# One float32 product per score tile, and one softmax and transpose group per pair, in the attention of a fused attention and two-layer expert kernel

## The chip, the cores and the metric

The kernel runs on one core of a Trainium2 chip. The core has a matrix engine (TensorE, in the rows PE, with its weight loads as PEld), a vector engine (DVE), an activation engine (ACT), GpSimd (POOL) and a queue engine (SP) that issues most transfers. The metric is device time in microseconds (us) for one launch; lower is better.

## The reference

The inputs are q, k and v of 8 batches, 8 heads, 576 positions and 64 channels in float32, and five weight matrices.

```
k_p = mean of k over groups of 8 positions      # 576 -> 72 keys
v_p = mean of v over groups of 8 positions
scores = q @ k_p.T / 8                          # per batch and head: 576 x 72
attn = softmax(scores)                          # over the 72 pooled keys
x = (attn @ v_p), heads side by side            # 4608 tokens x 512
h = max(x @ w1, x @ w2, x @ w3)                 # 4608 x 768
y = h @ w_out                                   # 4608 x 512
out = (max(y @ w_in, 0) ** 2) @ w_out2          # 2048 hidden units
```

## The kernel before

The work has two stages. The first holds the attention and the three-expert layer (`moe1`), for 12 blocks of 384 tokens (`T1`). The second, from about 776 us on, is the squared layer and is not touched by the change.

All large products are made from float32 numbers split into a high and a low part of a shorter type, float32r (`F32R`); a product of two split operands is three products of parts (`PARTS`). A `split` is a copy to float32r on ACT and a subtraction on DVE or POOL. `moe1(j)` issues 22 steps for block j (`STEPS`): 18 steps of 12 products of 384 columns (L487), then 4 steps of 18 products (L506). Three PSUM banks (`mm_ps`) take turns as their targets.

The attention of block j+1 is laid between the steps of block j. A block has pieces: the part of one batch in it, of 384 or 192 tokens (`n`). For each piece and each of the 4 pairs of heads, `attend` gives five functions, and `attention` puts each at a time in `todo`, counted in steps: `load` 10 steps ahead, `prepare` 4 steps ahead, `softmax`, then `transpose` 3 steps later (`LAG_T`), then `values` 3 steps after the last transpose (`LAG_V`). The list is sorted and recorded in that order, and a scheduler then sets each engine's own order. A piece of 384 tokens has 3 score tiles of 128 tokens, one of 192 has 2 tiles of 96 (`score_tiles`). Over the kernel there are 96 tiles of 128 and 64 tiles of 96.

- Batch 0 (`whole`, `b < NATURAL`): the scores are one float32 product a tile with `kbd_f` (L356).
- Batches 1 to 7: `prepare` splits q into `qs` and the pooled keys into `kbd` (L203), and a tile's scores are three float32r products of 144 columns (L360).
- In blocks 0 and 1 (`LIGHT`) all tiles of a piece go through one `softmax` group; in blocks 2 to 11 each tile is a group of its own.
- `softmax`: the maximum (DVE, L362), an exponential with its sum for each tile and head (ACT, L365), a sum guard and a reciprocal (DVE), and the scaling (POOL, L371).
- `transpose`: both heads of one tile are transposed on TensorE into one tile `tr` of its own PSUM bank, and written to `pt` by ACT (L396, high part) and DVE (L397, low part).
- `values`: each head's products with the pooled values go to the banks `av0` and `av1` (L417, L418), and x is formed and split.

Before the first steps can run at full rate, 18 tiles of `w1` and 6 of `wo1` are loaded and turned from 64-bit to float32 by two ACT and two DVE operations each (`wbits`, L149 to L154), and then split. Later blocks do the same for the second stage's weights.

Of the kernel before, what the change touches and what calls it, by code (L numbers as in the profile page):

```python
# [20 lines left out]
P = 128  # L21
# [47 lines left out]
LIGHT = 2  # L69
# [16 lines left out]
def attention_moe_kernel(ctx: ExitStack, tc: tile.TileContext, q, k, v, vn, w1, w2, w3, wo1, wi2, wo2, out):  # L86
# [90 lines left out]
    qs_p = s_at.enter_context(tc.tile_pool(name="qs_p", bufs=2, side="right"))  # L177
# [8 lines left out]
    kbd = kv_p.tile([P, NPAIR, 2, 2, SP], F32R, name="kbd")  # L186

    vst = kv_p.tile([SP, NPAIR, 4, D], F32R, name="vst")

    kbd_f = kv_p.tile([P, NPAIR, 2, SP], F32, name="kbd_f")  # L190
    nc.gpsimd.memset(kbd_f, 0.0)
# [5 lines left out]
    nc.gpsimd.memset(as_f32(kbd), 0.0)  # L197
# [28 lines left out]
    def prepare_k(b, p, kr):  # L226
        ks = sm_p.tile([P, SP], F32, tag="ks", name="ks", bufs=2)
        nc.vector.tensor_reduce(out=ks, in_=kr.rearrange("p (a b) -> p a b", b=POOL), axis=AX.X, op=ALU.add)
        for h in range(2):
            r = slice(h * D, (h + 1) * D)  # L230
            if b < NATURAL:
                nc.scalar.activation(kbd_f[r, p, h], ks[r], AF.Copy, scale=K_SCALE)
            else:
                split_scaled(kbd[r, p, 0, h], kbd[r, p, 1, h], ks[r], K_SCALE)
# [48 lines left out]
    def attention(j):  # L283

        x_t[j] = [None] * NPAIR
        n_tiles = sum(NPAIR * len(score_tiles(n)) for _, _, n, _ in pieces(j))
        pace = (STEPS - 1) / n_tiles
        at = (j - 1) * STEPS + pace / 2 - (LAG_T + LAG_V + LEAD_X)
        for b, s0, n, t in pieces(j):
            if s0 == 0 and b < NATURAL:  # L290
                tiles = []
                when = at - pace / 2 + LAG_T + LAG_V if t else at + pace / 2
                todo.append((when - LEAD_LOAD, lambda b=b, tiles=tiles: tiles.extend(load_natural(b))))
                todo.append((when, lambda tiles=tiles: pool_v(tiles)))
            for p in range(NPAIR):
                load, prepare, softmax, transpose, values = attend(j, b, s0, n, p, t)
                todo.append((at - LEAD_LOAD, load))
                todo.append((at - LEAD_PREP, prepare))
                tiles = score_tiles(n)
                if j < LIGHT:  # L300
                    todo.append((at, functools.partial(softmax, tiles)))
                for c, m in tiles:
                    if j >= LIGHT:
                        todo.append((at, functools.partial(softmax, [(c, m)])))
                    todo.append((at + LAG_T, functools.partial(transpose, c, m)))
                    at += pace
                todo.append((at - pace + LAG_T + LAG_V, values))
# [10 lines left out]
    def attend(j, b, s0, n, p, t):  # L318

        kr, vr, qr, qs, pt, sms = [], [], [], [], [], {}  # L320
        first, light, whole = s0 == 0, j < LIGHT, b < NATURAL

        def load():
# [7 lines left out]
            if j:  # L331
                qr.append(raw_p.tile([P, T1], F32, tag="qr", name="qr", bufs=2)[:, :n])
# [4 lines left out]
        def prepare():  # L337
            if first:
                prepare_k(b, p, kr[0])
            if whole:  # L340
                return
            qs.append(qs_p.tile([P, 2, T1], F32R, tag="qs", name="qs")[:, :, :n])
            split(qs[0], qr[0], nc.gpsimd if light else nc.vector)

        def softmax(tiles):

            c, m = tiles[0]
            if vr and (light or c == m):
# [5 lines left out]
            for i, (c, _) in enumerate(tiles):  # L354
                if whole:
                    nc.tensor.matmul(src[:, i], lhsT=qr[0][:, c : c + m], rhs=kbd_f[:, p], start=True, stop=True)  # L356
                    continue
                hi, lo = qs[0][:, 0, c : c + m], qs[0][:, 1, c : c + m]
                for n, (lhsT, l) in enumerate(((hi, 0), (hi, 1), (lo, 0))):
                    nc.tensor.matmul(src[:, i], lhsT=lhsT, rhs=kbd[:, p, l], start=(n == 0), stop=(n == 2))  # L360
# [14 lines left out]
            for i, (c, _) in enumerate(tiles):  # L375
                sms[c] = ss[:, i]

        def transpose(c, m):
            if c == 0 and whole:
                pt.append(pt_p.tile([SP, 2, T1], F32, tag="pt", name="pt"))  # L380
            elif c == 0:
                pt.append(pt_p.tile([SP, 2, 2, T1], F32R, tag="pt", name="pt"))
            if light and c == m:
                tr = av_ps.tile([P, T1], F32, tag="av1", name="tr")[:SP, : 2 * P].rearrange("s (h q) -> s h q", h=2)
            else:
                tr = tr_ps.tile([SP, 2, P], F32, tag="tr", name="tr")
            for h in range(2):
                nc.tensor.transpose(tr[:, h, :m], sms[c][:, h], ident[:m, :m])  # L388
            if whole:
                if p % 2:  # L390
                    nc.vector.tensor_copy(pt[0][:, :, c : c + m], tr[:, :, :m])
                else:
                    nc.scalar.activation(pt[0][:, :, c : c + m], tr[:, :, :m], AF.Copy)
                return
            hi, lo = pt[0][:, 0, :, c : c + m], pt[0][:, 1, :, c : c + m]
            nc.scalar.activation(hi, tr[:, :, :m], AF.Copy)  # L396
            nc.vector.tensor_tensor(out=lo, in0=tr[:, :, :m], in1=as_f32(hi), op=ALU.subtract)  # L397
# [355 lines left out]
```

## Time and profile before

| what | value |
|---|---|
| time, median of 3 runs | 1535.58 us (1532.88 to 1535.72) |
| profiled execution, first to last instruction (its span) | 1532.5 us |
| median beside that span | 3.1 us more |
| TensorE matmuls busy | 1502.5 us (98%) |
| DVE busy | 943.6 us (62%) |
| ACT busy | 618.6 us (40%) |
| POOL busy | 192.8 us (13%) |
| mean granted TensorE clock | 0.991 of full speed |

No time of the profiled execution is listed apart from its span; what the chip needs around it is read as the 3.1 us between the span and the median. "Busy" is a mean over the whole span; matmuls overlap in the pipeline, so a matmul's own duration is longer than the distance to the next one, and the distance is what counts for the rate.

### The profile page before, as it was taken

How to read it: one execution, taken by the hardware profiler on the slowest of the kernel's cores; microseconds unless marked ns; L12 is line 12 of the kernel's file. 1: busy time of each engine (PE TensorE's matmuls, PEld its weight loads, DVE VectorE, ACT ScalarE, POOL GpSimd, SP SyncE). 2: the span in 40 equal slices, each digit the busy share in tenths (PEclk: the TensorE clock that was granted, in tenths of full speed). 3: DMA queues.
4: the chain of work that ended last, by engine and by line, in shares of the span. 5: the costliest groups of instructions: out<-in, count | busy, mean ns of one | idle time of the engine just before them, and what ended most of it. 6: DMA issues, size and time to landing. Idle time of an engine off the chain costs nothing.

```text
span 1532.5 us, 25029 instructions
## 1 busy us (share of the span) xinstructions
PE 1502.5 (98%) x9254; PEld 1407.0 (92%) x9254; DVE 943.6 (62%) x1971; ACT 618.6 (40%) x1756; POOL 192.8 (13%) x329
## 2 busy tenths in 40 slices
PE   6889999999999999999999999999999999999998
PEld 4779999999999999999999899988999988999987
DVE  5897577776777766854427456464656555564644
ACT  6785466665666556654212112121212112121211
POOL 3551022222222221212000000000000000000000
PEclk8899999999999999999999999999999999999999
DMA  6553134333344333323485434333333433243321
GB/s 208 182 162 92 62 105 154 133 105 136 127 132 137 110 120 98 118 76 113 136 307 195 152 111 165 110 128 126 105 138 130 145 124 135 84 154 110 137 111 69
DMA packets 80858, 200.86 MB, mean 131 GB/s; under 512 B 9024, under 2 KB 32576, under 8 KB 80736
## 3 DMA queue, kind: packets, MB, share of 16 engines
q1 hardware_dynamic: 73824, 189.83, 36.3%
q10 hardware_dynamic: 6912, 9.44, 1.8%
q8 instruction: 73, 1.20, 0.3%
q14 instruction: 49, 0.40, 0.1%
HBM read 157.29 MB, written 41.94 MB: 130 GB/s over the span
## 4 chain that ended last, share of the span: by engine, by line
PE 88%; DVE 5%; DMA 3%; ACT 2%; issue 1%; SPq 0%; POOL 0%; ACTq 0%; DVEq 0%; POOLq 0%
PE acc L669 26%; PE ps L487 25%; PE ps L624 23%; PE ps L506 9%; PE sc L360 2%; PE tr L388 2%; DMA wraw<-in_wo_dram 1%; PE av L418 1%; PE av L417 1%; DVE wbits L151 1%; DVE wbits L154 1%; DMA wraw<-in_w_dram 1%; ACT ss L365 1%; DMA kq<-in_k_dram 1%; DMA vr<-in_v_dram 0%
## 5 line engine op out<-in xcount | busy, mean ns | idle before, releaser
L487 PE MATMUL ps<-x,w 128*128 128x384 f32 x2592 | 504.6, 342 | 2.1 <-DVE hm L495 1.7
L487 PEld LDWEIGHTS ps<-x,w 128*128 128x128 f32 x2592 | 448.7, 190 | 4.7 <-ACT wbits L149 2.0
L669 PE MATMUL acc<-wo2s,g 128*128 128x512 f32 x1728 | 411.0, 391 | 0.0
L624 PEld LDWEIGHTS ps<-y,wi2s 128*128 128x128 f32 x3024 | 368.9, 188 | 8.4 <-DVE c L641 0.5
L624 PE MATMUL ps<-y,wi2s 128*128 128x256 f32 x3024 | 374.1, 280 | 0.5 <-DVE c L641 0.3
L669 PEld LDWEIGHTS acc<-wo2s,g 128*128 128x128 f32 x1728 | 316.7, 188 | 62.9
L122 ACT ACTIVATE g<-c 128x512 fp32r<-128x512 f32 x144 | 90.7, 630 | 409.0 <-DVE c L635 399.7
L641 DVE TENSOR_TENSOR s<-ps,s 128x512 f32<-128x512 f32 x72 | 49.8, 691 | 253.7 <-PE ps L624 253.5
L506 PE MATMUL ps<-h,wo 128*128 128x384 f32 x864 | 168.1, 342 | 3.0 <-DVE st L369 0.9
L506 PEld LDWEIGHTS ps<-h,wo 128*128 128x128 f32 x864 | 149.9, 190 | 4.4 <-POOL wo L123 2.0
L371 POOL TENSOR_TENSOR ss<-ss,st 128x144 f32<-128x144 f32 (+3 forms) x144 | 71.4, 497 | 383.9 <-DVE st L370 297.7
L495 DVE TENSOR_TENSOR hm<-ps,hm 128x384 f32<-128x384 f32 x144 | 79.6, 553 | 60.6 <-PE ps L487 58.0
L641 DVE TENSOR_TENSOR c<-ps,s 128x512 f32<-128x512 f32 x144 | 99.0, 688 | 27.7 <-PE ps L624 24.4
L123 DVE TENSOR_TENSOR g<-c,g 128x512 fp32r<-128x512 f32 x144 | 98.7, 686 | 23.6 <-ACT g L122 22.9
L365 ACT ACTIVATE ss<-sc,st 128x72 f32<-128x72 f32 (+1 forms) x320 | 98.4, 314 | 35.2 <-DVE st L362 33.5
L635 DVE SCALAR_TENSOR_TENSOR c<-c 128x512 f32<-128x512 f32 x144 | 98.9, 688 | 2.2
L592 POOL COPY t<-g 1x1 f32<-1x1 f32 x32 | 8.4, 304 | 692.8 <-DVE g L123 692.8
L397 DVE TENSOR_TENSOR pt<-tr,pt 72x256 fp32r<-72x256 f32 (+1 forms) x140 | 54.0, 386 | 41.1 <-ACT pt L396 40.4
L396 ACT ACTIVATE pt<-tr 72x256 fp32r<-72x256 f32 (+1 forms) x140 | 49.3, 353 | 61.4 <-PE tr L388 59.6
L360 PE MATMUL sc<-kbd,qs 128*128 128x144 f32 (+1 forms) x420 | 65.1, 261 | 0.6 <-ACT ss L365 0.6
L362 DVE TENSOR_REDUCE st<-sc 128x2 f32<-128x144 f32 (+3 forms) x144 | 45.4, 316 | 32.9 <-PE sc L360 25.1
L122 ACT ACTIVATE h<-hm 128x384 fp32r<-128x384 f32 x72 | 37.7, 523 | 68.8 <-DVE hm L495 68.1
(84 smaller groups left out, 1349.5 us busy)
## 6 DMA issues: line engine op xcount, KB each, us to landing
wo2s<-wo_dram SPq DMA_DIRECT2D x144, 512.0 KB
wi2s<-wi_dram SPq DMA_DIRECT2D x24, 512.0 KB
wraw<-in_wo_dram SPq DMA_DIRECT2D x22, 512.0 KB
wraw<-in_w_dram SPq DMA_DIRECT2D x18, 512.0 KB
y_dram<-ys ACTq DMA_DIRECT2D x48, 192.0 KB
out_dram<-o SPq DMA_DIRECT2D x36, 256.0 KB
wraw<-in_wi_dram SPq DMA_DIRECT2D x16, 512.0 KB
wi_dram<-wraw SPq DMA_DIRECT2D x16, 512.0 KB
```

The lines of the kernel that those rows point to most:

```text
L122: nc.scalar.activation(hi, src, AF.Copy)
L123: engine.tensor_tensor(out=lo, in0=src, in1=as_f32(hi), op=ALU.subtract)
L360: nc.tensor.matmul(src[:, i], lhsT=lhsT, rhs=kbd[:, p, l], start=(n == 0), stop=(n == 2))
L365: nc.scalar.activation(ss[:, i, h], src[:, i, h], AF.Exp, bias=st[:, 0, i, h : h + 1], accum_out=st[:, 1, i, h : h + 1],)
L371: nc.gpsimd.tensor_tensor(out=ss, in0=ss, in1=st[:, 2].rearrange("p g (h o) -> p g h o", o=1).to_broadcast([m, g, 2, SP]), op=ALU.mult,)
L487: nc.tensor.matmul(ps, lhsT=w1_t[f, e][:, a, kk * P : (kk + 1) * P], rhs=x[kk][:, c], start=(n == 0), stop=(n == 3 * KD - 1),)
L495: nc.vector.tensor_tensor(out=hm, in0=ps, in1=hm, op=ALU.max)
L506: nc.tensor.matmul(ps, lhsT=wo1_t[kk][:, a, d * P : (d + 1) * P], rhs=hs[kk][:, c], start=(n == 0), stop=(n == 3 * KF1 - 1),)
L624: nc.tensor.matmul(bank[:, u * HT : (u + 1) * HT], lhsT=wi2_t[2 * gr + u][i][:, a, o + kk * P : o + (kk + 1) * P], rhs=y_t[j][m][:, c, kk] ...
L635: nc.vector.scalar_tensor_tensor(out=c, in0=c, scalar=0.0, in1=c, op0=ALU.max, op1=ALU.mult)
L641: nc.vector.tensor_tensor(out=c, in0=bank, in1=other, op=ALU.add)
L669: nc.tensor.matmul(acc_t[j][2 * half + i], lhsT=g[:, a, u * HT + i * P : u * HT + (i + 1) * P], rhs=wo2_t[j, 4 * gr + 2 * u + h][:, c], st ...
```

## The change

Every score tile, of every batch, is now one float32 product of q and the pooled keys as they stand; the splits of q (`qs`) and of the keys (the low part of `kbd`) are gone, and with them the pool `qs_p` and one of the two key tiles. q tiles (`qr`) are held until the scores are made and have four buffers in place of two. In all blocks the 3 or 2 tiles of a piece are one softmax group. The transposes of a piece are made together, head by head: head 0 of all tiles into the bank of `tr`, head 1 of all tiles into the bank that the value products of head 1 (`av1`) also use. Each head is then evicted to `pt` by one ACT and one DVE operation over the whole piece.

```diff
-    kbd = kv_p.tile([P, NPAIR, 2, 2, SP], F32R, name="kbd")
-    kbd_f = kv_p.tile([P, NPAIR, 2, SP], F32, name="kbd_f")
-    nc.gpsimd.memset(kbd_f, 0.0)
+    kbd = kv_p.tile([P, NPAIR, 2, SP], F32, name="kbd")
+    nc.gpsimd.memset(kbd, 0.0)
...
-            if b < NATURAL:
-                nc.scalar.activation(kbd_f[r, p, h], ks[r], AF.Copy, scale=K_SCALE)
-            else:
-                split_scaled(kbd[r, p, 0, h], kbd[r, p, 1, h], ks[r], K_SCALE)
+            nc.scalar.activation(kbd[r, p, h], ks[r], AF.Copy, scale=K_SCALE)
...
-                tiles = score_tiles(n)
-                if j < LIGHT:
-                    todo.append((at, functools.partial(softmax, tiles)))
-                for c, m in tiles:
-                    if j >= LIGHT:
-                        todo.append((at, functools.partial(softmax, [(c, m)])))
-                    todo.append((at + LAG_T, functools.partial(transpose, c, m)))
-                    at += pace
+                todo.append((at, softmax))
+                todo.append((at + LAG_T, transpose))
+                at += pace * len(score_tiles(n))
                 todo.append((at - pace + LAG_T + LAG_V, values))
...
-                qr.append(raw_p.tile([P, T1], F32, tag="qr", name="qr", bufs=2)[:, :n])
+                qr.append(raw_p.tile([P, T1], F32, tag="qr", name="qr", bufs=4)[:, :n])
...
-            if whole:
-                return
-            qs.append(qs_p.tile([P, 2, T1], F32R, tag="qs", name="qs")[:, :, :n])
-            split(qs[0], qr[0], nc.gpsimd if light else nc.vector)
...
-                if whole:
-                    nc.tensor.matmul(src[:, i], lhsT=qr[0][:, c : c + m], rhs=kbd_f[:, p], start=True, stop=True)
-                    continue
-                hi, lo = qs[0][:, 0, c : c + m], qs[0][:, 1, c : c + m]
-                for n, (lhsT, l) in enumerate(((hi, 0), (hi, 1), (lo, 0))):
-                    nc.tensor.matmul(src[:, i], lhsT=lhsT, rhs=kbd[:, p, l], start=(n == 0), stop=(n == 2))
+                nc.tensor.matmul(src[:, i], lhsT=qr[0][:, c : c + m], rhs=kbd[:, p], start=True, stop=True)
...
-        def transpose(c, m):
+        def transpose():
...
             for h in range(2):
-                nc.tensor.transpose(tr[:, h, :m], sms[c][:, h], ident[:m, :m])
...
+                if h:
+                    tr = av_ps.tile([P, T1], F32, tag="av1", name="tr")[:SP, :n]
+                else:
+                    tr = tr_ps.tile([SP, T1], F32, tag="tr", name="tr")[:, :n]
+                for i, (c, _) in enumerate(tiles):
+                    nc.tensor.transpose(tr[:, c : c + m], sms[0][:, i, h], ident[:m, :m])
+                if not whole:
+                    hi, lo = pt[0][:, 0, h, :n], pt[0][:, 1, h, :n]
+                    nc.scalar.activation(hi, tr, AF.Copy)
+                    nc.vector.tensor_tensor(out=lo, in0=tr, in1=as_f32(hi), op=ALU.subtract)
+                elif h:
+                    nc.vector.tensor_copy(pt[0][:, h, :n], tr)
+                else:
+                    nc.scalar.activation(pt[0][:, h, :n], tr, AF.Copy)
```

On TensorE, in the middle of the first stage (`sc` are scores, `tr` transposes, `ps` the products of `moe1`), before stands this:

```order
L487 MATMUL ps<-x,w_3_0_522 128x384 x4
L487 MATMUL ps<-x,w_3_1_543 128x384 x12
L360 MATMUL sc<-kbd,qs 128x144 x3
L487 MATMUL ps<-x,w_3_2_566 128x384 x4
L388 MATMUL tr<-ident,ss 72x128 x2
L487 MATMUL ps<-x,w_3_2_566 128x384 x8
L487 MATMUL ps<-x,w_4_0_595 128x384 x12
L360 MATMUL sc<-kbd,qs 96x144 x3
```

And with the change, in such a stretch of a like block:

```order
L465 MATMUL ps<-x,w_1_1_412 128x384 x12
L367 MATMUL tr<-ident,ss 72x128 x3
L465 MATMUL ps<-x,w_1_2_422 128x384 x12
L339 MATMUL sc<-kbd,qr 128x144 x3
L465 MATMUL ps<-x,w_2_0_445 128x384 x4
L367 MATMUL tr<-ident,ss 72x128 x3
L465 MATMUL ps<-x,w_2_0_445 128x384 x8
```

The three scores in a row were the parts of one tile and are now the three tiles of a piece; two transposes (the heads of a tile) are now three (one head of the three tiles).

On DVE, at the end of the conversion of the first layer's weights (`wbits`; the last row of either fence is the last of these 48 operations; `kbd` and `qs` are the splits of keys and q, `st` the softmax statistics), before stands this:

```order
L228 TENSOR_REDUCE ks<-kr 128x72
L151 SCALAR_TENSOR_TENSOR wbits<-wbits,wraw 128x512
L362 TENSOR_REDUCE st<-sc 128x2
L369 TENSOR_SCALAR st<-st 128x2
L123 TENSOR_TENSOR qs<-qr,qs 128x384
L238 TENSOR_REDUCE vs<-vr 72x128
L421 TENSOR_TENSOR xf<-av_1178,xf 64x192
L362 TENSOR_REDUCE st<-sc 128x2
L397 TENSOR_TENSOR pt<-tr,pt 72x2x128
L203 SCALAR_TENSOR_TENSOR kbd<-ks,kbd 64x72 x2
L154 SCALAR_TENSOR_TENSOR wbits<-wraw,wbits 128x512
```

And with the change:

```order
L230 TENSOR_REDUCE vs<-vr 72x128
L348 TENSOR_SCALAR st<-st 128x6
L153 SCALAR_TENSOR_TENSOR wbits<-wraw,wbits 128x512
L223 TENSOR_REDUCE ks<-kr 128x72
L399 TENSOR_TENSOR xf<-av_1203,xf 64x192
L349 RECIPROCAL st<-st 128x6
L371 TENSOR_TENSOR pt<-tr,pt 72x384
L150 SCALAR_TENSOR_TENSOR wbits<-wbits,wraw 128x512
L230 TENSOR_REDUCE vs<-vr 72x128
L122 TENSOR_TENSOR x<-xf,x 128x192
L153 SCALAR_TENSOR_TENSOR wbits<-wraw,wbits 128x512
```

The splits of keys and q are gone from between the conversions, the statistics come for six columns at a time, and more of the later attention (the x of a piece, the transposes' eviction) has moved ahead of the last conversion. Ahead of the last weight split on ACT stand 70 exponentials before and 80 with the change, and 8 copies of q to float32r before and none with the change.

On TensorE with the change, in a block of 192-token pieces, this is a stretch between two uses of the `av1` bank (`av1_2734` is a value product of head 1, `tr_2778` the transposes of head 1 of a later pair; both lie in that bank):

```order
L396 MATMUL av1_2734<-pt_2562,vst_168 128x192
L465 MATMUL ps_2828<-x_2238,w1_2_0_445 128x384 x3
L465 MATMUL ps_2828<-x_2402,w1_2_0_445 128x384 x3
L339 MATMUL sc_2846<-kbd_169,qr_2483 96x144 x2
L465 MATMUL ps_2870<-x_1944,w1_2_1_476 128x384 x3
L465 MATMUL ps_2870<-x_2087,w1_2_1_476 128x384 x3
L465 MATMUL ps_2870<-x_2238,w1_2_1_476 128x384 x3
L465 MATMUL ps_2870<-x_2402,w1_2_1_476 128x384 x3
L465 MATMUL ps_2887<-x_1944,w1_2_2_486 128x384 x2
L367 MATMUL tr_2778<-ident_63,ss_2666 72x96 x2
```

Between the last value product and the first transpose stand 20 products of 384 columns and two score products. Before, from block 2 on, `av1` held value products alone and the transposes took turns in the bank of `tr`.

## Rows read from the trace of the kernel before

**Rows 1.** Busy time, share of the span, instructions, by engine.

```profile
PE 1502.5 (98%) x9254; PEld 1407.0 (92%) x9254; DVE 943.6 (62%) x1971; ACT 618.6 (40%) x1756; POOL 192.8 (13%) x329
```

**Rows 2.** Three stretches: busy PE, PEld, DVE, ACT, POOL; clock, DMA share, GB/s.

```profile
0.00:140.00 140.00, 115.46 (x585) 99.01 (x586) 108.47 (x230) 100.92 (x335) 59.05 (x64) 0.90 0.56 172
140.00:754.00 614.00, 613.21 (x3789) 605.48 (x3788) 416.78 (x1089) 360.49 (x1160) 125.34 (x233) 1.00 0.35 117
754.00:1532.00 778.00, 773.84 (x4884) 702.55 (x4882) 418.31 (x652) 157.22 (x262) 8.45 (x32) 1.00 0.38 135
```

**Rows 3.** All that TensorE waited for, 140 to 725 us (total, times, longest).

```profile
PE tr L388 <- DVE pt L397: 0.7, 2, 0.4
```

**Rows 4.** Stretches of 10 us, 90 to 120 us, columns as in group 2.

```profile
90.00:100.00 10.00, 7.97 (x47) 7.33 (x46) 9.97 (x20) 7.42 (x21) 4.89 (x5) 1.00 0.49 156
100.00:110.00 10.00, 8.37 (x46) 6.84 (x44) 9.34 (x21) 8.53 (x26) 6.78 (x5) 1.00 0.49 137
110.00:120.00 10.00, 7.11 (x35) 5.80 (x35) 9.84 (x23) 6.96 (x29) 4.03 (x4) 0.85 0.42 114
```

**Rows 5.** Of what TensorE waited for, 0 to 140 us, one row.

```profile
PE ps L487 <- DVE hm L495: 1.7, 1, 1.7
```

**Rows 6.** TensorE groups by shape: busy, mean ns of one, idle before.

```profile
L360 PE MATMUL sc<-kbd,qs 128*128 128x144 f32 x252 | 41.6, 268 | 0.6 <-ACT ss L365 0.6
L360 PE MATMUL sc<-kbd,qs 128*96 128x144 f32 x168 | 23.5, 250 | 0.0
```

**Rows 7.** TensorE in order of time, three stretches: start, length, instructions.

```profile
195.10 2.32 PE L487 MATMUL ps<-x,w 128*128 128x384 f32 x12
197.26 0.45 PE L360 MATMUL sc<-kbd,qs 128*128 128x144 f32 x3
197.54 2.31 PE L487 MATMUL ps<-x,w 128*128 128x384 f32 x12
...
248.12 2.29 PE L487 MATMUL ps<-x,w 128*128 128x384 f32 x12
250.25 0.40 PE L360 MATMUL sc<-kbd,qs 128*96 128x144 f32 x3
250.48 1.26 PE L487 MATMUL ps<-x,w 128*128 128x384 f32 x6
...
734.85 29.39 PE L487 MATMUL ps<-x,w 128*128 128x384 f32 x168
```

**Rows 8.** TensorE in order of time, two groups of float32 scores.

```profile
15.73 0.90 PE L356 MATMUL sc<-kbd_f,kq 128*128 128x144 f32 x6
...
40.33 0.65 PE L356 MATMUL sc<-kbd_f,qr 128*96 128x144 f32 x4
```

**Rows 9.** The float32 scores' durations, min, median, max in ns.

```profile
L356 PE MATMUL sc<-kbd_f,kq x24: 286/286/580, 6.3 to 20.6; 128*128 128x144 f32 x24
```

**Rows 10.** DVE groups by shape, 0 to 125 us.

```profile
L203 DVE SCALAR_TENSOR_TENSOR kbd<-ks,kbd 64x72 fp32r<-64x72 f32 x12 | 5.8, 485 | 0.2
L123 DVE TENSOR_TENSOR qs<-qr,qs 128x384 fp32r<-128x384 f32 x5 | 3.4, 686 | 0.0
```

**Rows 11.** ACT in order of time: the exponentials of one tile.

```profile
307.04 0.32 ACT L365 ACTIVATE ss<-sc,st 128x72 f32<-128x72 f32 x1
...
307.35 0.31 ACT L365 ACTIVATE ss<-sc,st 128x72 f32<-128x72 f32 x1
```

**Rows 12.** DVE groups by shape, whole span.

```profile
L362 DVE TENSOR_REDUCE st<-sc 128x6 f32<-128x432 f32 x4 | 2.4, 608 | 5.7 <-PE sc L356 5.7
...
L238 DVE TENSOR_REDUCE vs<-vr 72x128 f32<-72x1024 f32 x28 | 33.9, 1211 | 3.4 <-DMA vr<-in_v_dram 3.0
...
L421 DVE TENSOR_TENSOR xf<-av,xf 64x384 f32<-64x384 f32 x56 | 31.0, 554 | 9.5 <-ACT xf L420 7.6
```

**Rows 13.** POOL's scaling of a group of three tiles, whole span.

```profile
L371 POOL TENSOR_TENSOR ss<-ss,st 128x432 f32<-128x432 f32 x4 | 3.6, 908 | 19.3 <-DVE st L370 19.3
```

**Rows 14.** ACT groups by shape, whole span.

```profile
L493 ACT ACTIVATE hm<-ps 128x384 f32<-128x384 f32 x72 | 34.9, 485 | 21.0 <-PE ps L487 20.2 <-ACT ss L365 0.4
```

More of the change, by code (lines that the diff above doesn't have):

```diff
@@ L67 @@
 NATURAL = 1
-LIGHT = 2
 REBIAS = 2.0**-112
@@ L176, in attention_moe_kernel @@
     raw_p = s_at.enter_context(tc.tile_pool(name="raw_p", bufs=4, side="right"))
-    qs_p = s_at.enter_context(tc.tile_pool(name="qs_p", bufs=2, side="right"))
     sm_p = s_at.enter_context(tc.tile_pool(name="sm_p", bufs=4, side="right"))
@@ L196, in attention_moe_kernel @@
         vst_f.append(vf)
-    nc.gpsimd.memset(as_f32(kbd), 0.0)
     K_SCALE = 1.0 / (POOL * D**0.5)
@@ L224, in load_v, with prepare_k @@
         return vr
-    def prepare_k(b, p, kr):
+    def prepare_k(p, kr):
         ks = sm_p.tile([P, SP], F32, tag="ks", name="ks", bufs=2)
@@ L318, in attend @@
     def attend(j, b, s0, n, p, t):
-        kr, vr, qr, qs, pt, sms = [], [], [], [], [], {}
-        first, light, whole = s0 == 0, j < LIGHT, b < NATURAL
+        kr, vr, qr, pt, sms = [], [], [], [], []
+        first, whole = s0 == 0, b < NATURAL
         def load():
@@ L338, in prepare, with softmax @@
             if first:
-                prepare_k(b, p, kr[0])
-            if whole:
-                return
-            qs.append(qs_p.tile([P, 2, T1], F32R, tag="qs", name="qs")[:, :, :n])
-            split(qs[0], qr[0], nc.gpsimd if light else nc.vector)
-        def softmax(tiles):
-            c, m = tiles[0]
-            if vr and (light or c == m):
+                prepare_k(p, kr[0])
+        tiles = score_tiles(n)
+        m = tiles[0][1]
+        def softmax():
+            if vr:
                 prepare_v(p, vr.pop())
@@ L374, in softmax @@
             )
-            for i, (c, _) in enumerate(tiles):
-                sms[c] = ss[:, i]
-        def transpose(c, m):
-            if c == 0 and whole:
+            sms.append(ss)
+        def transpose():
+            if whole:
                 pt.append(pt_p.tile([SP, 2, T1], F32, tag="pt", name="pt"))
-            elif c == 0:
+            else:
                 pt.append(pt_p.tile([SP, 2, 2, T1], F32R, tag="pt", name="pt"))
[L383 to L386, printed above, removed]
             for h in range(2):
-                nc.tensor.transpose(tr[:, h, :m], sms[c][:, h], ident[:m, :m])
-            if whole:
-                if p % 2:
-                    nc.vector.tensor_copy(pt[0][:, :, c : c + m], tr[:, :, :m])
-                else:
[L393 to L397, printed above, removed]
+                if h:
+                    tr = av_ps.tile([P, T1], F32, tag="av1", name="tr")[:SP, :n]
+                else:
+                    tr = tr_ps.tile([SP, T1], F32, tag="tr", name="tr")[:, :n]
[9 more added lines that the diff above has]
+                    nc.scalar.activation(pt[0][:, h, :n], tr, AF.Copy)
         def values():
```

## Prediction

> **What bounds the kernel now.** First the page's busy line: TensorE works on matmuls for 98% of the span, its weight loads for 92%, DVE for 62% [rows 1]. These are means, so the second view is busy time by stretch [rows 2]. From 140 to 754 us TensorE is busy for 613.2 of 614 us at a granted clock of 1.00; DVE has 197 us to spare there and ACT 254 us. The second stage, 773.8 of 778 us, is not touched. The list of waits says the same from the other side: from 140 to 725 us TensorE waited 0.7 us in all [rows 3]. So in the first stage after its start only a TensorE instruction removed, or a new wait of TensorE, moves the end; DVE, ACT and POOL work that goes away there is worth nothing by itself.
>
> The first 140 us are another matter: TensorE is idle for 24.5 us and its mean granted clock is 0.90 [rows 2]. From 90 to 120 us DVE is busy for 29.15 of 30 us, while TensorE idles for 6.55 us [rows 4], and one of its waits there is for a DVE maximum, 1.7 us [rows 5]. In that stretch DVE work that goes away can be worth time.
>
> **The score products, the first term.** There are 252 and 168 float32r products [rows 6], three a tile: 84 tiles of 128 and 56 of 96 (the other 20 tiles are batch 0's and already float32). A product's own duration, 250 to 268 ns, isn't its price, since matmuls overlap. I take the price from ends in order of time. Plain `moe1` products are (29.39 - 0.34) / 167 = 0.174 us apart, 0.34 being one product's length [rows 7]. Around a 128 tile, the 12 products before end at 197.42 and the 12 after at 199.85: 2.43 less 12 x 0.174 leaves 0.34 us for three score products. Around a 96 tile, ends at 250.41 and 251.74 leave 1.33 less 6 x 0.174, 0.29 us [rows 7]. So the old price is 84 x 0.34 + 56 x 0.29 = 44.8 us; the rounding of the rows, 0.01 a tile, makes it 43.4 to 46.2.
>
> A float32 product shows as two records. Six of them, three tiles, take 0.90 us of which the last lasts 0.286 [rows 8, 9]: (0.90 - 0.286) / 5 = 0.123 apart, 0.246 us a tile. A 96 tile costs the same: (0.65 - 0.286) / 3 = 0.121 [rows 8]. The new price is 140 x 0.245 = 34.3 us.
>
> That frees 46.2 - 34.3 = 11.9 us at the most. What these rows don't show is the change from a `moe1` product to a float32 score and back in a run without stalls. For 96-wide scores in float32r, the three cost 0.29, not three times an inner spacing, so an edge can cost something like 0.03 us. At 56 groups that is up to 1.7 us, and with the low rounding the gain is at least 43.4 - 34.3 - 1.7 = 7.4 us. I take **9.2 us**, between the ends, since groups of three have fewer edges than single tiles had.
>
> The page "FP8 and Floating Point Precision" of the Trainium skill (TensorE Precision Notes) says that true float32 takes 4 passes through the array, while the reduced form is float32 read and cut to a 22-bit number. Taken as a price, four passes against three would make the new scores dearer by a third; by that the term would be a loss and not a gain. The float32 rows agree with four passes (0.246 us a tile), but the three float32r products cost 0.34 and not three quarters of that, so in this trace the rule's other half doesn't hold at 144 columns.
>
> **The transposes** keep their number and shape on TensorE, 320 of them; only their order changes. I cost them at nothing. Their evictions are fewer and longer; DVE and ACT have the room just named after 140 us. The same room hides the regrouped softmax, the dropped splits of q and of the keys, and the longer hold of q, whose loads are 10 steps ahead. If that cover were gone (an engine late by more than the distance in TensorE's order), each would cost its lateness; that is the third term.
>
> **The start, the second term.** Up to 125 us DVE spends 5.8 us on key splits and 3.4 us on q splits [rows 10], 9.2 us that go. ACT loses 8 q copies ahead of the last weight split but gains 10 exponentials at 0.31 us a piece, the distance of two starts (307.35 - 307.04) [rows 11]: about 3.1 us more against some 4 us less, near nothing. The order on DVE shows that the freed places are in part taken by later attention ahead of the last weight conversion. At best the 6.55 us of idle time from 90 to 120 us go; at worst the added exponentials make the last weights 3 us late. I take **2 us gained**, a third of the idle time, as part of the freed work only lets other work forward.
>
> **New waits, the third term.** A group of three tiles takes, after its products, a maximum of 0.61 us [rows 12], six exponentials of 6 x 0.31 = 1.9, a scaling of 0.91 [rows 13] and two small DVE operations, some 4 us with the hops. In the new order of TensorE at least 6.7 us of work stand between a group's scores and its first transpose after the start, except for one group of the last attended block at 4.9. What can be late next is the `av1` bank. After head 1's transposes it is free when ACT and DVE have evicted it: 0.49 [rows 14] plus 0.55 for a 384-column DVE operation from PSUM [rows 12], 1.04 us. In the stretch shown, the distance to its next use is 20 x 0.174 + 2 x 0.245 = 3.97 us, and typical ones are 3.7 to 4.0. That is enough unless both engines are behind by over 2.7 us. Behind a transpose that waits stand all `moe1` products, and for these everything. The bounds are 0 and 3 us (three places at block edges stand nearer, each perhaps 1 us); I take **0.5 us lost**.
>
> **Sum.** 1532.5 - 9.2 - 2 + 0.5 = 1521.8 us for the span. The median of the runs stands 3.1 us above the span, so the time is 1524.9, **1525 us**. All best bounds together give 1535.6 - 11.9 - 6.5 = 1517.2, all worst ones 1535.6 - 7.4 + 3 + 3 = 1534.2; this case alone I hold to 1520 to 1530.
>
> **The rivals.**
>
> The start gives more. If the 9.2 us of DVE work come off one to one (the idle time of 90 to 120 us and part of the 0.90 clock, since idle stretches go with the lower clock there), the time is 1535.6 - 9.2 - 9.2 + 0.5 = 1517.7. For it: DVE is full there. Against: ACT is 70 to 85% full in the same stretch, and weights still come in by DMA.
>
> The gain is given back. The larger groups keep ACT from the weights in the start, and the bank of `av1` waits now and then: 9.2 gained, 3 lost at the start, 4 to 8 in waits, 1533 to 1537. For it: 10 more exponentials stand ahead of the last weights. Against: 0.7 us of waits before, with an order made by the same scheduler.
>
> The `av1` bank decides, and the kernel gets slower. A second-head eviction behind six exponentials on ACT (1.9 us) and behind one reduction of values on DVE (1.21 [rows 12]) frees the bank after 1.9 + 1.21 + 1.04 = 4.15 us, 0.2 later than the 3.97 wanted. At two uses a piece, 112 in blocks 1 to 11, that is 22 us: 1535.6 - 11.2 + 22 = 1546. It decides from 11.2 / 112 = 0.1 us a use on. For it: before, `av1` held no transposes after the start. Against: both collisions would have to fall on every use.
>
> Float32 is dearer in the run than in the start. If the parts of a float32r product really cost three quarters of a float32 one, 0.184 us a tile, the new scores would add 140 x 0.061 = 8.6 us: 1535.6 + 8.6 - 2 + 0.5 = 1543. Against it stand the ends in [rows 7]; only a fault in that reading would leave it. The page named above is where it comes from.
>
> **How the numbers follow.** The likeliest case 0.65, the start gives more 0.13, given back 0.11, the bank decides 0.08, dearer float32 0.03. A change of 0.2% (3 us) is about what a measurement of this kernel can tell from none. Faster than 1532.5 are the first two: 0.78; the third is the same, 0.11; the last two are slower, 0.11. The range from 1517 to 1535 holds the first two and half of the third, and leaves out the last two; the likeliest alone has 1520 to 1530.
>
> **What would show it.** In the new profile, three score tiles between two runs of `moe1` products should add 0.74 to 0.77 us by ends. TensorE from 140 us to the end of the first stage should stay over 99% busy, with waits under 3 us, and that stretch should end some 11 us earlier. From 90 to 120 us, DVE below 97% or TensorE's idle time below 6.5 us would bear out the second term. Waits of transposes or value products for DVE `pt` or `xf` of more than 10 us in all would make the forecast wrong, as would a start that is longer than 140 us or has a lower clock.

## The result, and the profile after

The changed kernel takes 1521.78 us (median of 4 runs, 1519.51 to 1523.94) against 1535.65 (4 runs, 1532.88 to 1535.95). The ratio is 0.9914, with a 95% interval from 0.99 to 0.9928: 13.9 us faster, where 10.7 were forecast. The profiled execution took 1521.07 us with a span of 1519.0, 13.5 less than the span of before.

The page's busy line of the changed kernel answers to [rows 1]:

```profile
span 1519.0 us, 23903 instructions
...
PE 1488.1 (98%) x9114; PEld 1397.0 (92%) x9114; DVE 876.3 (58%) x1593; ACT 591.2 (39%) x1670; POOL 171.3 (11%) x244
```

By itself it does not show where the gain comes from: every engine does less, and TensorE is at 98% in both. The end of each stage is read from the lines of the second stage's first product. Its first and last start on TensorE are the numbers behind the shape's durations, of the kernel before:

```profile
L624 PE MATMUL ps<-y,wi2s x3024: 276/279/389, 776.6 to 1517.1; 128*128 128x256 f32 x189
```

and of the changed kernel:

```profile
L602 PE MATMUL ps<-y,wi2s x3024: 276/279/388, 762.6 to 1503.2; 128*128 128x256 f32 x189
```

The first stage is 14.0 us shorter. From there to the end it is 1532.5 - 776.6 = 755.9 us before and 756.4 after, so the second stage gave nothing. Busy time by stretch of the changed kernel (columns as in [rows 2]), with the three slices that answer to [rows 4]:

```profile
0.00:140.00 140.00, 114.40 (x600) 99.43 (x601) 101.87 (x202) 105.61 (x362) 52.95 (x54) 0.93 0.56 180
140.00:743.00 603.00, 602.73 (x3652) 597.93 (x3651) 356.81 (x740) 328.80 (x1049) 109.87 (x158) 1.00 0.35 117
...
90.00:100.00 10.00, 8.91 (x53) 7.79 (x51) 9.90 (x20) 8.20 (x25) 4.65 (x4) 1.00 0.40 129
100.00:110.00 10.00, 7.47 (x35) 6.76 (x34) 7.13 (x13) 8.48 (x26) 4.83 (x4) 0.83 0.35 119
110.00:120.00 10.00, 7.69 (x46) 6.90 (x46) 8.77 (x16) 5.61 (x12) 6.12 (x5) 1.00 0.40 117
```

From 140 us on TensorE idles for 0.27 us in 603. All its waits there, to 725 us, in the view that answers to [rows 3]:

```profile
PE ps L465 <- ACT hm L471: 0.2, 1, 0.2
```

No transpose and no value product waits for a bank or an eviction. The score tiles stand between `moe1` products like this (TensorE in order of time, as [rows 7]):

```profile
302.03 1.42 PE L465 MATMUL ps<-x,w 128*128 128x384 f32 x7
303.29 0.90 PE L339 MATMUL sc<-kbd,qr 128*128 128x144 f32 x6
303.93 1.84 PE L465 MATMUL ps<-x,w 128*128 128x384 f32 x9
```

The ends are 303.45 and 305.77; 2.32 less 9 x 0.174 is 0.75 us for three tiles. Over all ten places in the trace where such a group stands alone between `moe1` products, the median is 0.734, or 0.245 a tile; for groups of two 96 tiles, again ten places, it is 0.489, also 0.245 a tile. The same reading of the kernel before, over 51 and 37 places, gives 0.334 a 128 tile and 0.283 a 96 tile. The score products are therefore 84 x (0.334 - 0.245) + 56 x (0.283 - 0.245) = 7.5 + 2.1 = 9.6 us cheaper.

The rest of the 14.0 us shows when the work done by 140 us is counted. TensorE's groups by shape from 0 to 140 us, of the kernel before:

```profile
L487 PE MATMUL ps<-x,w 128*128 128x384 f32 x284 | 61.5, 364 | 2.1 <-DVE hm L495 1.7 <-POOL w L123 0.2
L506 PE MATMUL ps<-h,wo 128*128 128x384 f32 x72 | 16.8, 374 | 3.0 <-DVE st L369 0.9 <-DVE hm L495 0.9 <-ACT wo L122 0.7
...
L388 PE MATMUL tr<-ident,ss 128*72 128x128 f32 x36 | 7.7, 323 | 0.9 <-DVE pt L391 0.6 <-DVE pt L397 0.3
L360 PE MATMUL sc<-kbd,qs 128*128 128x144 f32 x35 | 7.1, 302 | 0.6 <-ACT ss L365 0.6
...
L360 PE MATMUL sc<-kbd,qs 128*96 128x144 f32 x24 | 3.4, 292 | 0.0
...
L417 PE MATMUL av<-pt,vst 72*128 72x384 f32 x2 | 0.9, 568 | 0.0
```

and of the changed kernel:

```profile
L465 PE MATMUL ps<-x,w 128*128 128x384 f32 x275 | 59.7, 366 | 5.0 <-POOL w L122 5.0
L484 PE MATMUL ps<-h,wo 128*128 128x384 f32 x72 | 15.2, 352 | 0.5 <-ACT ys L490 0.5
L367 PE MATMUL tr<-ident,ss 128*72 128x128 f32 x51 | 8.3, 295 | 4.3 <-POOL ss L350 2.7 <-DVE xf L399 1.6
L339 PE MATMUL sc<-kbd,qr 128*128 128x144 f32 x46 | 7.9, 302 | 1.4 <-ACT ss L344 1.4
...
L395 PE MATMUL av<-pt,vst 72*128 72x384 f32 x5 | 2.1, 418 | 0.7 <-DVE xf L399 0.4 <-DVE pt L371 0.3
```

By 140 us the old kernel had made 35 / 3 = 11.7 tiles of 128 of the split kind, the new one 46 / 2 = 23. So it is ahead by 11.3 tiles (11.3 x 0.245 = 2.8 us), 15 transposes (0.110 each where two stand between `moe1` products, 1.7) and 3 value products of 384 columns for each head (two take 0.353, so 1.1), and behind by 9 `moe1` products (1.6): 3.9 us of TensorE work. Of that, 11.7 x 0.089 + 8 x 0.038 = 1.3 is what the start's own score tiles became cheaper by, and is in the 9.6 already. The start is worth **2.6 us** beside it. It isn't less idle time: TensorE idles for 25.6 us in the first 140, and did for 24.5. But the mean granted clock there is 0.93 and was 0.90. All this compares one execution of each kernel; runs of the same kernel lie up to 4.4 us apart.

What is left, 14.0 - 9.6 - 2.6 = 1.8 us, lies after 140 us: waits of 0.2 us where there were 0.7 [rows 3], and `moe1` products that stand closer together. Over the whole stretch what they take beyond 0.174 each sums to 0.6 us and did to 2.4; it collects in the second to fifth product behind a piece of attention work, and there are 175 such runs of products where there were 234. The two make 2.3 us; the count above is no finer than that.

### The profile page after: what moved, and what is told of

It is laid out like the page before. It is cut to its first block, busy times and chain, and to the rows that moved or that the text cites. A ratio compares the mean times of both kernels' runs of the same rounds, so it can differ in the third digit from the quotient of the medians.

```text
span 1519.0 us, 23903 instructions
## 1 busy us (share of the span) xinstructions
PE 1488.1 (98%) x9114; PEld 1397.0 (92%) x9114; DVE 876.3 (58%) x1593; ACT 591.2 (39%) x1670; POOL 171.3 (11%) x244
## 4 chain that ended last, share of the span: by engine, by line
PE 92%; ACT 3%; DMA 2%; DVE 2%; issue 1%; POOL 0%; DVEq 0%; ACTq 0%; SPq 0%; POOLq 0%
PE ps L465 27%; PE acc L647 26%; PE ps L602 23%; PE ps L484 9%; PE sc L339 2%; PE tr L367 2%; ACT ss L344 1%; DMA vr<-in_v_dram 1%; PE av L396 1%; PE av L395 1%; DMA wraw<-in_w_dram 0%; ACT wbits L148 0%; ACT wraw L149 0%; DVE wbits L153 0%; PE vp L252 0%
## 5 line engine op out<-in xcount | busy, mean ns | idle before, releaser
L465 PE MATMUL ps<-x,w 128*128 128x384 f32 x2592 | 494.4, 341 | 5.3 <-POOL w L122 5.0
L484 PE MATMUL ps<-h,wo 128*128 128x384 f32 x864 | 162.0, 339 | 0.5 <-ACT ys L490 0.5
L350 POOL TENSOR_TENSOR ss<-ss,st 128x432 f32<-128x432 f32 (+1 forms) x64 | 56.8, 888 | 261.7 <-DVE st L349 179.7
L399 DVE TENSOR_TENSOR xf<-av,xf 64x192 f32<-64x192 f32 (+1 forms) x112 | 50.7, 453 | 47.8 <-ACT xf L398 45.9
L371 DVE TENSOR_TENSOR pt<-tr,pt 72x192 fp32r<-72x192 f32 (+1 forms) x112 | 49.6, 449 | 38.2 <-ACT pt L370 36.7
L398 ACT ACTIVATE xf<-av 64x192 f32<-64x192 f32 (+1 forms) x112 | 45.4, 405 | 54.1 <-PE av L396 38.7
L344 ACT ACTIVATION_READ_ACCUMULATOR ss<-sc,st 128x1 f32 (+1 forms) x320 | 66.2, 207 | 0.0
```

Source lines behind the costliest of these rows:

```text
L344: nc.scalar.activation(ss[:, i, h], src[:, i, h], AF.Exp, bias=st[:, 0, i, h : h + 1], accum_out=st[:, 1, i, h : h + 1],)
L350: nc.gpsimd.tensor_tensor(out=ss, in0=ss, in1=st[:, 2].rearrange("p g (h o) -> p g h o", o=1).to_broadcast([m, g, 2, SP]), op=ALU.mult,)
L399: nc.vector.tensor_tensor(out=xf[r], in0=av[r], in1=xf[r], op=ALU.add)
L465: nc.tensor.matmul(ps, lhsT=w1_t[f, e][:, a, kk * P : (kk + 1) * P], rhs=x[kk][:, c], start=(n == 0), stop=(n == 3 * KD - 1),)
L484: nc.tensor.matmul(ps, lhsT=wo1_t[kk][:, a, d * P : (d + 1) * P], rhs=hs[kk][:, c], start=(n == 0), stop=(n == 3 * KF1 - 1),)
```

## The experiments

Medians are of the runs made with each kernel; each ratio is to the kernel before on the same chip (medians 1534.07 to 1534.69 there), with its 95% interval.

| kernel | median us | ratio | second stage begins |
|---|---|---|---|
| the change again | 1520.58 | 0.9909 (0.9895 to 0.9922) | 762.8 |
| float32 scores, groups as before | 1526.07 | 0.9943 (0.993 to 0.9955) | 768.4 |
| groups of the change, split scores | 1531.3 | 0.9982 (0.9973 to 0.999) | 772.8 |
| change, scores twice | 1545.76, one run | none | 787.7 |
| change, DVE work of the start put back | 1522.82 | 0.9929 (0.9915 to 0.9942) | 764.8 |
| the same four times over | 1529.54 | 0.997 (0.9958 to 0.9982) | 770.6 |
| change, transposes tile by tile | 1529.0 | 0.9964 (0.9952 to 0.9977) | 771.0 |
| change, high parts of scores only | 1513.45 | 0.9863 (0.9849 to 0.9876) | 755.1 |
| the same, attention laid 4 steps earlier | 1506.02 | 0.9818 (0.9802 to 0.9834) | 747.5 |
| change, attention laid 4 steps earlier | 1515.9 | 0.9881 (0.9866 to 0.9895) | 758.3 |

**The two halves of the change.** One kernel takes only the float32 product, and with it the splits of q and the keys go:

```diff
-                if whole:
-                    nc.tensor.matmul(src[:, i], lhsT=qr[0][:, c : c + m], rhs=kbd_f[:, p], start=True, stop=True)
-                    continue
-                hi, lo = qs[0][:, 0, c : c + m], qs[0][:, 1, c : c + m]
-                for n, (lhsT, l) in enumerate(((hi, 0), (hi, 1), (lo, 0))):
-                    nc.tensor.matmul(src[:, i], lhsT=lhsT, rhs=kbd[:, p, l], start=(n == 0), stop=(n == 2))
+                nc.tensor.matmul(src[:, i], lhsT=qr[0][:, c : c + m], rhs=kbd_f[:, p], start=True, stop=True)
```

> Only the scores change: one float32 product a tile, no splits of q and keys; softmax groups, transposes and evictions stay as they were. Two theories on the 13.9 us that the change gained. A: 9.6 us are TensorE time of score products (84 tiles x 0.089 + 56 x 0.037), and some 4 us are gained in the first 140 us because the splits are gone from DVE. B: the 9.6 us are the same, but the 4 us come from the grouping of softmax and transposes. A expects 1521 to 1523 us, as the change; B expects 1525 to 1527 us.

The other takes only the grouping, with the splits and the three products kept:

```diff
-                for c, m in tiles:
-                    if j >= LIGHT:
-                        todo.append((at, functools.partial(softmax, [(c, m)])))
-                    todo.append((at + LAG_T, functools.partial(transpose, c, m)))
-                    at += pace
+                todo.append((at, softmax))
+                todo.append((at + LAG_T, transpose))
+                at += pace * len(score_tiles(n))
```

> Only the grouping changes: one softmax group a piece in all blocks, transposes and evictions by head; the scores keep their splits and three float32r products. A (the splits in the start carry the 4 us) expects the time of the kernel before, 1534 to 1537 us. B (the grouping carries them) expects 1530 to 1533 us. A third view, that the shared bank of head 1 costs TensorE waits which the dropped splits hide in the change, expects more than 1538 us.

Both times, 1526.07 and 1531.3 us, lie in the ranges of theory B, which gave the 4 us to the grouping. The traces show that both theories had a part of it.

Together the two kernels make 0.9943 x 0.9982 = 0.9925, against 0.9914 and 0.9909 for the change: nearly all of it, and what is over is no more than the intervals. The scores alone gain 8.4 us, the first stage 8.2, less than the 9.6 that their products became cheaper by. Yet this kernel, in which DVE's splits are gone too, gains more in the start than the change does. Its `moe1` products done by 140 us:

```profile
L471 PE MATMUL ps<-x,w 128*128 128x384 f32 x321 | 67.5, 357 | 3.8 <-ACT x L122 2.0 <-DVE hm L479 0.7 <-POOL w L123 0.7
```

That is 37 more than before, 6.4 us, and it is 2.3 score tiles of 128 ahead, 0.6 us, with the other attention even. Less the 1.3 us that is in the 9.6 already, its start is worth 5.7 us. So 15.3 us were to be gained in the first stage, and 7.1 of them were lost again after 140 us. Its waits of TensorE from 140 to 760 us say where:

```profile
PE sc L344 <- ACT ss L349: 2.5, 3, 1.2
PE tr L372 <- DVE pt L381: 1.5, 2, 0.9
```

and its busy time in the two stretches where most of them fall, with the eighth of the columns, the clock, below 1.00, and in 2 us of the first one:

```profile
470.00:500.00 30.00, 27.85 (x165) 27.00 (x164) 21.62 (x63) 20.11 (x77) 7.52 (x15) 0.94 0.50 162
660.00:690.00 30.00, 28.71 (x163) 27.36 (x162) 18.93 (x50) 16.50 (x53) 6.41 (x11) 0.94 0.17 62
...
486.00:488.00 2.00, 2.00 (x8) 2.00 (x7) 1.86 (x6) 0.82 (x3) 0.43 (x1) 0.50 0.38 107
```

A score tile there waits for the exponentials of an earlier tile, and a transpose for an eviction: 4.0 us, 3.3 more than before. On top of it comes the granted clock of 0.94 over twice 30 us, as if 2 x 30 x 0.06 = 3.6 us were lost. That makes 6.9 of the 7.1 us. The grouping alone has no such waits:

```profile
140.00:740.00 600.00, 600.00 (x3723) 596.13 (x3722) 391.79 (x835) 349.54 (x1111) 109.36 (x159) 1.00 0.35 119
```

TensorE is busy for 600.00 of 600 us. Its start is worth next to nothing, 0.2 us by the same count, with DVE as busy there as before (108.77 us, and 108.47 [rows 2]), and its first stage is 3.8 us shorter. The 0.7 us of waits are gone, what the `moe1` products take beyond 0.174 each falls from 2.4 to 0.7 us, and longer runs are a little cheaper: four 96-wide transposes in a row cost 0.362 us in the changed kernel, and two runs of two cost 2 x 0.197 before.

So the gain in the start comes with the scores' half of the change and not with the grouping. The grouping takes away the waits that faster scores bring out, and in the change only 2.6 of the 5.7 us in the start are left. ACT has more to do in the start of the change, 105.61 us against 99.88 in the kernel with the scores alone; whether that is the reason, and whether grouping after the start only would keep both gains, was not tried.

**The price of the float32 product, by doubling it.** Each score product of the changed kernel is made twice over:

```diff
             for i, (c, _) in enumerate(tiles):
-                nc.tensor.matmul(src[:, i], lhsT=qr[0][:, c : c + m], rhs=kbd[:, p], start=True, stop=True)
+                for _ in range(2):
+                    nc.tensor.matmul(src[:, i], lhsT=qr[0][:, c : c + m], rhs=kbd[:, p], start=True, stop=True)
```

> The change, with every float32 score product issued twice into the same place (the result is the same). If TensorE is the bound after the start and a product's price there is 0.245 us, the 109 tiles scored after 140 us add 26.7 us, and the 51 in the start add between nothing and 12.5 us: 1548 to 1561 us. If the scores were hidden behind another engine, the time would stay near 1522 us.

Its one run, 1545.76 us, is under the 1548 to 1561 us expected. The second stage begins 787.7 - 762.6 = 25.1 us later. TensorE's busy time from 140 us to there, and its score groups by shape in that stretch:

```profile
140.00:787.00 647.00, 647.00 (x3985) 643.47 (x3984) 363.22 (x752) 337.13 (x1071) 109.31 (x159) 1.00 0.33 111
...
L340 PE MATMUL sc<-kbd,qr 128*128 128x144 f32 x266 | 39.8, 286 | 0.0
L340 PE MATMUL sc<-kbd,qr 128*96 128x144 f32 x192 | 28.4, 285 | 0.0
```

The stretch is full. Two records are a product and half of the products are the added ones: 458 / 4 = 114.5, which at 0.245 cost 28.1 us. The start had done 28 `moe1` products more (4.9 us less to do here), which is why the time is under the range; what helped the start isn't shown. The last 25.1 - 28.1 + 4.9 = 1.9 us are attention work that it had not got to: 5.5 score tiles (1.3), 9 transposes (1.0) and 2 value products for each head (0.7), together 3.0, so that the count is right to about 1 us of 28. Read directly, the two places where eight records of 128 stand between `moe1` products add 0.979 us, 0.245 a product. So the new price, read in the start, holds in the full run.

**The start, by putting DVE's work back.** The changed kernel gets a subtraction of q per piece of block 2 and a split-like operation per head for the keys of batches 1 and 2, whose outputs nothing uses:

```diff
+            if 0 < b < 3:
+                nc.vector.scalar_tensor_tensor(
+                    out=kl[r], in0=ks[r], scalar=K_SCALE, in1=kbd[r, p, h], op0=ALU.mult, op1=ALU.subtract
+                )
...
+            if j == 2:
+                nc.vector.tensor_tensor(out=ql[:, :n], in0=qr[0], in1=qr[0], op=ALU.subtract)
```

> The change, with the DVE work of the start put back as idle work: 16 operations of the size of a key split for batches 1 and 2 and 4 of the size of a q split in block 2, into scratch tiles that nobody reads, about 8 us of DVE. If DVE time in the start carried the 4 us, the time goes back by 2 to 4 us, to 1524 to 1526 us. If the start's part is the granted clock, which differs from run to run, the time stays at 1520 to 1523 us.

The other kernel has both operations four times over:

> The change with four times the idle DVE work of the run before in the start (64 small operations of key-split size and 16 of q-split size, some 33 us of DVE in the first 140 us). If DVE time is what the start waits for, most of it must show, as DVE had only some 38 us to spare in the first 140 us: 1532 to 1550 us. If the start hangs on the chains through ACT, POOL and DMA instead, it is mostly absorbed: 1522 to 1528 us.

Busy time from 0 to 140 us of the change run again, of the kernel with the work once, and with it four times, one row each:

```profile
0.00:140.00 140.00, 113.95 (x599) 98.04 (x600) 103.05 (x203) 105.67 (x364) 53.52 (x54) 0.94 0.57 180
```

```profile
0.00:140.00 140.00, 110.19 (x587) 93.19 (x588) 110.35 (x212) 100.37 (x343) 57.23 (x53) 0.96 0.56 178
```

```profile
0.00:140.00 140.00, 109.02 (x551) 94.59 (x552) 122.49 (x253) 102.55 (x354) 61.63 (x54) 0.90 0.52 171
```

DVE has 7.3 and 19.4 us more to do, TensorE gets to 12 and 48 fewer instructions, and the kernels are 2.2 and 9.0 us slower than the change run again. The first step is within the two intervals, and 1522.82 us lies in the range that was named for the granted clock, not for DVE. But the clock of its start is not lower: it is 0.96, against 0.94, and TensorE is idle there for 29.8 us, against 26.1. The second step is well outside the intervals, and its 1529.54 us falls between the two ranges: DVE work in the start costs time, but less than half of it shows. Both steps together give 0.3 to 0.5 us per microsecond of DVE work. DVE's busy time there fell from 108.47 [rows 2] to 101.87 by the change, 6.6 us, which at that rate makes 2 to 3 us, an estimate of the size of the start's 2.6. It is not a rule for every order: the float32 scores alone gained 5.7 us in the start with DVE at 104.10. And POOL's busy time there fell too, from 59.05 [rows 2] to 52.95; its part wasn't tried.

**What the transposes by head do.** The changed kernel with its softmax groups, but each tile transposed on its own into the bank of `tr` and evicted on its own, as before:

```diff
-                todo.append((at + LAG_T, transpose))
-                at += pace * len(score_tiles(n))
+                for c, m in score_tiles(n):
+                    todo.append((at + LAG_T, functools.partial(transpose, c, m)))
+                    at += pace
```

> The change with the transposes and evictions a tile at a time again, in the bank of tr alone after the start, as before; float32 scores and one softmax group a piece stay. In the run with only the scores changed TensorE waited 4 us after 140 us, for the score bank's exponentials and for the transposes' eviction, and lost half of its clock twice. If the grouped softmax is what removes these waits, this is as fast as the change, 1520 to 1523 us. If the transposes by head in two banks remove them, the waits for pt stay and it takes 1524 to 1527 us.

It is 8.4 us slower than the change run again, slower than either range, and by the medians slower even than the float32 scores alone. Its waits of TensorE from 140 to 745 us, and a stretch in which some of them fall:

```profile
PE tr L367 <- DVE pt L376: 2.2, 3, 1.5
PE ps L466 <- ACT x L121: 1.1, 2, 0.9
PE sc L340 <- ACT ss L345: 0.7, 1, 0.7
PE av L396 <- ACT pt L375: 0.5, 1, 0.5
...
480.00:500.00 20.00, 18.48 (x108) 17.26 (x107) 13.51 (x30) 12.68 (x49) 2.06 (x4) 0.91 0.40 123
```

The waits are 4.5 us, and the clock of 0.91 over 20 us is as if another 1.8 were lost. Both are gone when the transposes are made by head and use two banks, `av1` among them: the grouped softmax alone doesn't take the waits away. This run can't tell apart the second bank, the fewer evictions and the order.

**The change again.** The unedited kernel, beside the others:

> The change itself, once more, beside the three others on the same chip: 1519 to 1524 us, for the spread of its start from run to run and as the mark for the others.

Its 1520.58 us, 0.9909, repeat the result, and its second stage begins at 762.8 us, as in the change's first profile.

**Less TensorE work still.** Here the scores of batches 1 to 7 are one float32r product a tile: the low parts of q and of the keys are left out of them, and ACT makes the rounded q (which gets three buffers, and q two again).

```diff
+            if not whole:
+                qs.append(qs_p.tile([P, T1], F32R, tag="qs", name="qs")[:, :n])
+                nc.scalar.activation(qs[0], qr[0], AF.Copy)
...
-                nc.tensor.matmul(src[:, i], lhsT=qr[0][:, c : c + m], rhs=kbd[:, p], start=True, stop=True)
+                nc.tensor.matmul(src[:, i], lhsT=(qr if whole else qs)[0][:, c : c + m], rhs=(kbd_f if whole else kbd)[:, p], start=True, stop=True)
```

> The change, but batches 1 to 7 score with one float32r product a tile of q and keys rounded by ACT (the low parts of the scores are left out). If a float32r product costs what it cost before, 0.111 us for a 128 tile and 0.094 for one of 96, and TensorE is the bound after the start, the 109 tiles scored after 140 us give back 61 x 0.134 + 48 x 0.151 = 15.4 us, all 140 tiles 19.7 us: 1502 to 1507 us. If a narrow product had a floor near the float32 one, or another engine were the bound, it stays above 1515 us.

It gains 7.1 us on the change run again, and 1513.45 us lies in neither range. The longest of its waits from 140 to 745 us, 3.6 of 6.6 us in all, and a stretch of it:

```profile
PE tr L373 <- DVE xf L405: 3.6, 3, 1.3
...
480.00:500.00 20.00, 20.00 (x109) 19.64 (x110) 16.41 (x32) 13.98 (x48) 6.01 (x8) 0.92 0.25 88
```

A transpose that waits for DVE's `xf`, the reader of `av1`, is the slower rival's mechanism. It is real, and it comes when TensorE gets through its work faster, not in the change. The next two kernels, this one and the change, lay all attention 4 steps further ahead of the block that uses it:

```diff
-LEAD_LOAD, LEAD_PREP, LAG_T, LAG_V, LEAD_X = 10, 4, 3, 3, 4
+LEAD_LOAD, LEAD_PREP, LAG_T, LAG_V, LEAD_X = 10, 4, 3, 3, 8
```

> The run with the scores' high parts alone (their low parts left out), with the attention of a block laid 8 steps ahead of its use instead of 4. That run waited 6.4 us after 140 us, in places where attention stands close together at a block's edge, and lost half of its clock for 3.4 us there. If the waits are a matter of too little lead, they go and the time falls by 5 to 8 us, to 1505 to 1509 us. If they come from the bank that head 1's transposes share with its value products, more lead moves them but leaves them: 1511 to 1515 us.

> The change with the attention laid 8 steps ahead instead of 4. After 140 us the change has 0.3 us of waits, so there is nothing to win there: 1519 to 1523 us. If in the start the attention's place decides (it comes earlier among the weights' conversions), the time moves by more than 3 us, and up.

With the low parts left out, the lead takes all waits after 140 us away and 7.4 us with them, as expected of too little lead: the bank is as shared as it was, and 1506.02 us is in the range that the price alone gave the run before. The change itself had next to no waits to lose after 140 us and still gains 4.7, which was not expected: the range was 1519 to 1523 us, and a move, if any, was to be upwards. Its busy time in the start, and the `moe1` products it has done by 140 us:

```profile
0.00:140.00 140.00, 116.54 (x616) 100.53 (x617) 107.97 (x205) 104.81 (x362) 55.09 (x54) 0.94 0.57 179
...
L465 PE MATMUL ps<-x,w 128*128 128x384 f32 x299 | 63.8, 358 | 6.8 <-POOL w L122 4.4 <-ACT w L121 1.5 <-DVE x L122 0.4
```

299 against 275, and the 72 of the second kind in both: 24 x 0.174 = 4.2 us. Less 3 score tiles and 2 transposes that it is behind by (0.9), the start gains 3.3 of the 4.3 us by which the second stage begins earlier; where the last microsecond comes from isn't shown. DVE is busy there for 107.97 us, 6.1 more than in the change, so its busy time alone does not set the start either. With the whole computation this is the fastest kernel of the study, 1515.9 us, 0.9881 of the kernel before.

## Why the prediction was right, and where its sizes were off

**The score products** were forecast at 9.2 us and are 9.6 by the ends of the whole trace; doubling them bears out the new price. By the rows shown, three tiles add 0.75, inside the 0.74 to 0.77 named; the median over all places is a little under it. The edge that could cost up to 1.7 us isn't there: 0.734 for a group of three is three times 0.245. The page "FP8 and Floating Point Precision" of the Trainium skill (TensorE Precision Notes) counts four passes for a true float32 product. At the rate of the plain products, 0.174 us for 384 columns, 144 columns take 0.065 us, and 0.245 is 3.8 times that: the trace comes near that count. But three float32r products took 0.334 and not 3 x 0.065, so the count of passes doesn't give the price at this width.

**The start** was forecast at 2 us and is worth 2.6. The size was right, and in part by luck, as the account of it was not. It was to come out of the idle time from 90 to 120 us, and that fell from 6.55 to 5.93 us in one execution and to 4.70 in the change run again, while DVE fell to 9.90 + 7.13 + 8.77 = 25.80 of 30. But over the whole start TensorE is not less idle; what came instead is more work done by 140 us at a higher mean clock. The runs with DVE's work put back show that DVE work there costs time. The link to the clock is read from the rows and wasn't tried by itself, and the kernel with that work once, which has 0.96 and gets less done, shows that the clock alone does not decide. In the kernel with the scores alone the start is worth 5.7 us, and with the grouping 3 of them are gone; the forecast has no term for that.

**New waits** were the step that failed: 0.5 us lost was forecast, and 1.8 gained came. The argument from distances, 1.04 us of evictions in 3.7 to 4.0 us, held for `av1`: waits fell from 0.7 to 0.2 us. What the term had at nothing is that fewer and longer runs of attention work let the `moe1` products behind them stand closer, 2.4 us over the plain distance before and 0.6 now, and that longer runs of 96-wide transposes are a little cheaper. It also left out what the grouping was needed for: in the old order, tile by tile, faster scores alone bring out 4.0 us of waits and twice a lower clock.

The three terms make 9.6 + 2.6 + 1.8 = 14.0 for the first stage where 10.7 was the forecast; the second stage took 0.5 back. All three came out better than forecast, so no error hid another. The median stands 1521.78 - 1519.0 = 2.8 us over the span, where 3.1 was taken; the profiled execution itself took 2.1 us more than its span, and the rest is that the median is of other runs.

**The rivals.** The start giving more, 9.2 us one to one, falls: the start gave 2.6, and DVE work put back costs 0.3 to 0.5 a microsecond. The gain given back falls: no waits, no longer start. The `av1` bank deciding falls for this kernel, as its transposes waited for nothing after 140 us. Dearer float32 in the run falls too: by it the float32 scores alone would have lost 8.6 us, and they gained 8.4.

## What to carry to other kernels

Price a narrow product by the ends around it, not by its own duration and not by a count of passes: three short products can cost more than one float32 product. When an engine that bounds the kernel gets faster in one place, look at what its neighbours do per piece, since waits that were just covered come out; fewer and longer groups, over two banks, kept them covered here. Count the work done by a fixed time before calling a half of a change worthless: the scores alone gained 5.7 us in the start and lost 7.1 behind it. And where TensorE is full in the run, the start is where the next gain lies: laying the attention 4 steps earlier was worth 4.7 us by the medians, most of it there.

## What was not expected of the hardware

- Narrow float32r products cost more than their columns. At the plain rate 144 columns would be 0.065 us; three products with 128 columns of weights cost 0.334 us, 0.111 each, and three with 96 cost 0.283, six in a row 0.535 (one place before, and 0.537 over ten places of the kernel with the grouping alone), 0.089 each. A float32 product of the same 144 columns, two records, costs 0.245 at either width of weights. So the float32r price is lower with the narrower weights, at two widths; what makes it wasn't tried. The transposes, with 72 columns of weights, don't line up with that: 0.110 for 128 columns.
- Short waits at block edges came with a lower granted clock in the kernel with float32 scores alone. TensorE waited 0.9 and 1.2 us between 480 and 484 us, and from 486 to 488 us the granted clock was 0.50, the lower of its two levels, though TensorE was busy for all of those 2 us. Over the 30 us around it is 0.94, so that a wait cost more than its length.
- Of work that is added to DVE in the start of the changed kernel, only 0.3 to 0.5 reaches the end, though DVE was busy for 101.87 of 140 us there, and for 9.90 of the 10 us from 90 us on.
